# Two rows to a strided product, V laid out with keys adjacent, and softmax scaling moved to ScalarE in a fused attention and two-layer kernel

## The chip, the cores and the metric

The kernel runs on one core of a Trainium2 chip. The metric is the device time of one execution in microseconds. A kernel is run several times and the median is taken; one further execution is recorded by the hardware profiler, and its trace is what the rows below come from. Engines are named PE (TensorE, matmuls), PEld (its weight loads), DVE (VectorE), ACT (ScalarE), POOL (GpSimd) and SP (SyncE, which issues the DMAs here).

## What is computed

Attention on 4 batches, 8 heads, 576 positions, head size 64, and behind it two feed-forward layers on 2304 tokens of 512 values with 2048 hidden units, all in float32. The mask of the first four heads is local, that of the last four strided.

```
scores = (q @ k.T) / sqrt(64)
local  = (rel >= 0) & (rel < 32)                  # heads 0 to 3, rel = query - key
strided = (rel >= 0) & (key % 32 == query % 32)   # heads 4 to 7
attn = exp(where(mask, scores, -1e9) - max); attn /= (sum + 1e-9)
x  = attn @ v                                     # heads side by side: 2304 x 512
y1 = relu(x @ w_in1) ** 2 @ w_out1
h  = y1 @ w_in2;  g = max(h, 0) + alpha * min(h, 0)
out = g @ w_out2
```

## The kernel before

The 2304 tokens form six tiles of 384. Layer 1 goes through tiles 0 to 5, then layer 2 through tiles 0 to 5. A tile has 16 steps, one for each block of 128 hidden units. Matmuls keep float32 precision by splitting a number into a high and a low part (`xh` and `xl`, `gh` and `gl`, two parts of each weight), three products instead of one.

In step n of layer 1, `emit_h(n + 1)` multiplies the next block's first layer into the one PSUM bank `h` (12 matmuls), and `emit_y(n)` multiplies block n's second layer into four banks, first the eight matmuls with `gh`, then the four with `gl`. Between them ScalarE takes `h` out: relu into `g` (line 546), its square as `gh` (547) and once more in full as `g` (548). VectorE makes `gl = g - gh` (line 562). TensorE's next `h` waits for the relu, because there is one bank, and the second part of `y` waits for `gl`.

While the matmuls of tile t run, the attention of tile t + 1 is worked off piece by piece; `plan` and the tables at the top of the file say in which step each piece is emitted. Within a step the order is loads, `emit_gl(n)`, the list `front`, `emit_h(n + 1)`, the list `fill`, the list `tensor_part`, `emit_g(n + 1)`, the list `tail_part`, `emit_y(n)`. The scheduler of the framework may still reorder VectorE's and TensorE's instructions by readiness; SP's order is as written, and ScalarE's too from tile 1's steps on. At the last step `evac` takes the four banks of `y` out, two by ScalarE, two by VectorE.

*Local heads.* A `Unit` handles two heads and three blocks of 64 queries; a tile has four units, put at steps 0, 3, 6 and 9 (in tile 0 at 0, 4, 6 and 9). Its stages are `scores` (TensorE), `softmax_a` (VectorE: mask, maximum, times -scale), `softmax_b` one step later (ScalarE: exp with a sum on the side), `softmax_c` another step later (VectorE: sum plus epsilon, reciprocal, scaling), then `turn`, `turn_copy`, `values` and the emission of `xh` and `xl`. Tile 0's units and its `Dense` units, which do the strided heads of tile 0 by matmul, run ahead of the first step and have buffers of their own.

*Strided heads.* With stride 32 a query sees only the keys of its own residue, at most 18. Residue and head lie on the 128 partitions, and a `Strided` group works on VectorE alone: for a query row i it multiplies the row of q with i + 1 key rows of 64 and sums each product (`score_mul`, `score_sum`), takes the softmax of all rows at once, and multiplies and sums with V (`value_mul`, `value_sum`). In a tile from 2 on a group has 12 rows, i from 6 to 17; tile 1 has two groups, of two rows in two batches and of four rows in two batches. `pieces` cuts a row with more than 9 keys in two; the halves' value sums are then added. `parts` pairs the pieces (two products, then two sums) and `put_strided` spreads the pairs over 14 steps by an estimated cost. V lies in the DRAM as key by key, 64 values each, so that the value product reads operand 0 with keys 64 numbers (256 bytes) apart.

In tile 0's steps VectorE and ScalarE also convert the weights of layer 1 (lines 135 to 163); the last conversion ahead of a step's `h` is line 163.

Of the kernel before, what the change touches and what calls it, by code (L numbers as in the profile page):

```python
# [16 lines left out]
P = 128  # L17
D = 64
# [39 lines left out]
def attn_moe_moe2(  # L58
# [119 lines left out]
    class Unit:  # L178
# [29 lines left out]
        def softmax_a(self):  # L208
            self.e = self.new("e", [P, 3, 96], bufs=1)
            self.st = apool.tile([P, 3, 3], F32, tag="st", name="stat", bufs=4)  # L210
            s = self.s[:, 0:288].rearrange("p (n c) -> p n c", c=96)
            j = 0
            while j < 3:
                k = j
                while k < 3 and self.first[k] == self.first[j]:
                    k += 1
                m = mfirst if self.first[j] else mloc
                nc.vector.tensor_tensor(
                    out=self.e[:, j:k, :], in0=s[:, j:k, :],
                    in1=m.unsqueeze(1).to_broadcast([P, k - j, 96]), op=ALU.add,  # L220
                )
                j = k
            nc.vector.tensor_reduce(out=self.st[:, 0, :], in_=self.e, op=ALU.max, axis=AX.X)
            nc.vector.tensor_scalar(
                out=self.st[:, 0, :], in0=self.st[:, 0, :], scalar1=-SCALE, scalar2=None, op0=ALU.mult
            )

        def softmax_b(self):
            for j in range(3):
                nc.scalar.activation(  # L230
                    out=self.e[:, j, :], in_=self.e[:, j, :], func=AF.Exp, scale=SCALE,
                    bias=self.st[:, 0, j:j + 1], accum_out=self.st[:, 1, j:j + 1],
                )
# [44 lines left out]
    class Dense:  # L278
# [24 lines left out]
        def softmax_a(self):  # L303
            self.e = self.b["e"]
            self.st = apool.tile([P, 3, 3], F32, tag="st", name="stat", bufs=4)
            ms = (mstr.unsqueeze(1), mstr[:, 64:128].unsqueeze(1).to_broadcast([P, 2, 64]))
            for e, sc, m in zip(self.parts(self.e), self.parts(self.s), ms):
                nc.vector.tensor_tensor(out=e, in0=sc, in1=m, op=ALU.add)
            for e, st in zip(self.parts(self.e), (self.st[:, 0, 0:1], self.st[:, 0, 1:3])):
                nc.vector.tensor_reduce(out=st, in_=e, op=ALU.max, axis=AX.X)  # L310
            nc.vector.tensor_scalar(
                out=self.st[:, 0, :], in0=self.st[:, 0, :], scalar1=-SCALE, scalar2=None, op0=ALU.mult
            )

        def softmax_b(self):
            for j, (c, n) in enumerate(SPANS):
                nc.scalar.activation(
                    out=self.e[:, c:c + n], in_=self.e[:, c:c + n], func=AF.Exp, scale=SCALE,
                    bias=self.st[:, 0, j:j + 1], accum_out=self.st[:, 1, j:j + 1],
                )  # L320
# [49 lines left out]
    class Strided:  # L370
# [15 lines left out]
        def load_kv(self, kind):  # L386
            t = spool.tile([P, self.nb, self.a1, D], F32, tag="kv", name="kv", bufs=3)
            src = ks if kind == "k" else vs
            nc.sync.dma_start(
                out=t, in_=src[self.b0:self.b0 + self.nb, :, 0:self.a1, :].rearrange("b p a d -> p b a d")  # L390
            )
            setattr(self, kind, t)
# [4 lines left out]

        def pieces(self, i):

            n = i + 1  # L400
            if self.nb * n <= KCH:
                return [(0, self.nb, 0, n)]
            cuts = [(0, n)] if n <= KCH else [(0, n // 2), (n // 2, n)]
            return [(b, 1, j0, j1) for b in range(self.nb) for j0, j1 in cuts]

        def score_mul(self, i, b, nb, j0, j1):
            n, r = j1 - j0, i - self.a0
            pr = spool.tile([P, nb, n, D], F32, tag="pr", name="pr", bufs=2)
            kb, qb = self.k[:, b:b + nb, j0:j1, :], self.q[:, b:b + nb, r, :]
            if nb == 1:  # L410
                nc.vector.tensor_tensor(  # L411
                    out=pr[:, 0], in0=kb[:, 0],
                    in1=qb.to_broadcast([P, n, D]), op=ALU.mult,
                )
            else:
                nc.vector.tensor_tensor(
                    out=pr, in0=kb, in1=qb.unsqueeze(2).to_broadcast([P, nb, n, D]), op=ALU.mult
                )
            return pr

        def score_sum(self, pr, i, b, nb, j0, j1):
            r = i - self.a0
            if nb == 1:
                nc.vector.tensor_reduce(out=self.s[:, b, r, j0:j1], in_=pr[:, 0], op=ALU.add, axis=AX.X)  # L424
            else:
                nc.vector.tensor_reduce(out=self.s[:, b:b + nb, r, j0:j1], in_=pr, op=ALU.add, axis=AX.X)

        def wide(self, x):
            return x.unsqueeze(2).to_broadcast([P, self.nb * self.n, self.a1])

        def softmax_a(self):
            s = self.s.rearrange("p b n a -> p (b n) a")
# [16 lines left out]

        def value_mul(self, i, b, nb, j0, j1):  # L450
            n, r = j1 - j0, i - self.a0
            pr = spool.tile([P, nb, D, n], F32, tag="pr", name="pr", bufs=2)
            vb, pb = self.v[:, b:b + nb, j0:j1, :], self.s[:, b:b + nb, r, j0:j1]
            if nb == 1:
                nc.vector.tensor_tensor(  # L455
                    out=pr[:, 0], in0=vb[:, 0].rearrange("p a d -> p d a"),
                    in1=pb.to_broadcast([P, D, n]), op=ALU.mult,
                )
            else:
                nc.vector.tensor_tensor(  # L460
                    out=pr, in0=vb.rearrange("p b a d -> p b d a"),
                    in1=pb.unsqueeze(2).to_broadcast([P, nb, D, n]), op=ALU.mult,
                )
            return pr

        def value_sum(self, pr, i, b, nb, j0, j1):
            r = i - self.a0
            if nb > 1:
                nc.vector.tensor_reduce(out=self.o[:, b:b + nb, r, :], in_=pr, op=ALU.add, axis=AX.X)
                return  # L470
            o = self.o[:, b, r, :]
            if j0 == 0:
                nc.vector.tensor_reduce(out=o, in_=pr[:, 0], op=ALU.add, axis=AX.X)  # L473
            else:
                o2 = self.q[:, b, r, :]
# [24 lines left out]
        def parts(self):  # L500

            ps = []
            for kind, mul, add in (
                ("k", self.score_mul, self.score_sum), ("v", self.value_mul, self.value_sum)
            ):
                todo = [(i, pc) for i in range(self.a0, self.a1) for pc in self.pieces(i)]
                for j in range(0, len(todo), 2):

                    def fn(mul=mul, add=add, mine=todo[j:j + 2]):
                        prs = [mul(i, *pc) for i, pc in mine]  # L510
                        for pr, (i, pc) in zip(prs, mine):
                            add(pr, i, *pc)

                    ps.append((sum(134 * pc[1] * (pc[3] - pc[2]) + 140 for _, pc in todo[j:j + 2]), fn, kind))
                if kind == "k":
# [74 lines left out]
    def evac(t, layer):  # L590
# [300 lines left out]
```

## Time and profile before

| | |
|---|---|
| median of 3 runs | 925.78 us (921.92 to 926.69) |
| profiled execution | 927.54 us, of which the recorded span is 925.7 us |
| PE busy | 885.2 us (96%) |
| DVE busy | 613.1 us (66%), 1153 instructions |
| ACT busy | 423.7 us (46%), 939 instructions |
| POOL busy | 1.5 us |

Busy time is the union of an engine's instructions. Matmuls overlap and their ends are modelled, so a busy PE is not one at its peak; a share over the whole span is a mean over stages with different limits. Layer 2 fills the span from 519 us on.

### The profile page before, as it was taken

The page shows a single profiled execution, that of the slowest core. Times are in us where ns is not written, and L with a number is a line of the kernel's source. Part 1 is how long each engine was busy: PE and PEld are TensorE (multiplying, and loading weights), DVE is VectorE, ACT ScalarE, POOL GpSimd, SP SyncE. Part 2 cuts the span into 40 slices and gives each one's busy share as a digit, 9 for nine tenths or more (in the row PEclk, how much of TensorE's full clock was granted, in tenths as well). Part 3 has the DMA queues.
Part 4 walks back from the last instruction along what each step waited for, and adds up shares of the span by engine and source line. Part 5 has one row for each costly group of instructions (what it writes and reads, how often), then busy time and mean ns, then how long its engine had stood idle before and what let it go on. Part 6 is the DMA issues. An engine that isn't in the chain of part 4 may idle for free.

```text
span 925.7 us, 12898 instructions
## 1 busy us (share of the span) xinstructions
PE 885.2 (96%) x4956; PEld 826.6 (89%) x4956; DVE 613.1 (66%) x1153; ACT 423.7 (46%) x939; POOL 1.5 (0%) x10
## 2 busy tenths in 40 slices
PE   7888799989999998999999999999999999999998
PEld 6778689989998998999899999999999999898996
DVE  4899999898898989989578886323233333333222
ACT  4776544434444443543367665333333333434332
POOL 0000000000000000000000000000000000000000
PEclk9999799999999999999999999999999999999999
DMA  9936120213111201210278600100100100100000
GB/s 312 377 123 240 64 71 35 69 33 89 47 54 52 83 22 50 71 55 1 77 255 282 242 4 5 60 10 1 60 10 1 61 9 1 59 9 1 35 1 35
DMA packets 31933, 70.93 MB, mean 77 GB/s; under 512 B 5504, under 2 KB 16256, under 8 KB 31872
## 3 DMA queue, kind: packets, MB, share of 16 engines
q1 hardware_dynamic: 31872, 70.11, 22.2%
q8 instruction: 39, 0.64, 0.3%
q14 instruction: 22, 0.18, 0.1%
HBM read 60.66 MB, written 9.44 MB: 76 GB/s over the span
## 4 chain that ended last, share of the span: by engine, by line
PE 74%; DVE 20%; issue 2%; DMA 1%; ACT 1%; SPq 1%; ACTq 0%
PE ps_h L535 36%; PE ps_y L586 34%; DVE pr L455 7%; DVE so L473 2%; DVE sq L476 2%; DVE gl L562 2%; DVE wt L147 1%; PE ps_s L203 1%; DMA wraw<-in_w1i_dram 1%; DVE w L163 1%; DVE wt L144 1%; PE ps_pt L246 1%; PE ps_y L348 1%; DVE so L477 1%; DMA dense_qk<-in_qd_dram 1%
## 5 line engine op out<-in xcount | busy, mean ns | idle before, releaser
L535 PE MATMUL ps_h<-xh,w 128*128 128x384 f32 x1536 | 433.3, 343 | 7.9 <-ACT w L157 3.3
L535 PEld LDWEIGHTS ps_h<-xh,w 128*128 128x128 f32 x1536 | 287.3, 192 | 15.5 <-ACT w L157 4.4
L535 PE MATMUL ps_h<-xl,w 128*128 128x384 f32 x768 | 262.0, 341 | 0.0
L553 DVE SCALAR_TENSOR_TENSOR g<-u,nalpha,g 128x384 f32<-128x384 f32 x96 | 59.3, 618 | 193.6 <-ACT u L552 193.6
L562 DVE TENSOR_TENSOR gl<-g,gh 128x384 fp32r<-128x384 f32 x192 | 106.3, 553 | 76.6 <-ACT gh L556 49.1
L586 PE MATMUL ps_y<-gh,w 128*128 128x384 f32 x768 | 155.1, 343 | 0.0
L535 PEld LDWEIGHTS ps_h<-xl,w 128*128 128x128 f32 x768 | 147.3, 192 | 4.1
L546 ACT ACTIVATE g<-ps_h 128x384 f32<-128x384 f32 x96 | 47.2, 492 | 224.4 <-PE ps_h L535 208.4
L586 PE MATMUL ps_y<-w,gh 128*128 128x512 f32 x576 | 149.0, 394 | 0.1
L586 PEld LDWEIGHTS ps_y<-gh,w 128*128 128x128 f32 x768 | 135.3, 191 | 1.1
L551 ACT ACTIVATE g<-ps_h 128x384 f32<-128x384 f32 x96 | 47.2, 492 | 168.3 <-PE ps_h L535 168.1
L586 PEld LDWEIGHTS ps_y<-w,gh 128*128 128x128 f32 x576 | 106.6, 188 | 17.3 <-ACT gh L556 0.6
L586 PE MATMUL ps_y<-gl,w 128*128 128x384 f32 x384 | 85.5, 344 | 16.1 <-DVE gl L562 16.1
L586 PEld LDWEIGHTS ps_y<-gl,w 128*128 128x128 f32 x384 | 68.6, 192 | 20.2 <-DVE gl L562 20.0
L455 DVE TENSOR_TENSOR pr<-kv,ss 128x384 f32<-128x384 f32 (+4 forms) x92 | 85.1, 949 | 0.1
L556 ACT ACTIVATE gh<-g 128x384 fp32r<-128x384 f32 x96 | 50.5, 526 | 69.0 <-DVE g L553 69.0
L586 PE MATMUL ps_y<-w,gl 128*128 128x512 f32 x288 | 82.0, 392 | 0.0
L586 PEld LDWEIGHTS ps_y<-w,gl 128*128 128x128 f32 x288 | 54.1, 188 | 12.5
L411 DVE TENSOR_TENSOR pr<-kv,sq 128x384 f32<-128x384 f32 (+4 forms) x92 | 54.8, 616 | 0.0
L424 DVE TENSOR_REDUCE ss<-pr 128x6 f32<-128x384 f32 (+4 forms) x92 | 53.3, 611 | 0.1
L547 ACT ACTIVATE gh<-g 128x384 fp32r<-128x384 f32 x96 | 50.5, 526 | 3.0
L548 ACT ACTIVATE g<-g 128x384 f32<-128x384 f32 x96 | 50.5, 526 | 2.9
(103 smaller groups left out, 654.6 us busy)
## 6 DMA issues: line engine op xcount, KB each, us to landing
wraw<-in_w1i_dram SPq DMA_DIRECT2D x16, 512.0 KB, 7.7
wraw<-in_w1o_dram SPq DMA_DIRECT2D x16, 512.0 KB, 7.8
wraw<-in_w2i_dram SPq DMA_DIRECT2D x16, 512.0 KB, 3.6
wraw<-in_w2o_dram SPq DMA_DIRECT2D x16, 512.0 KB, 4.5
qk<-in_qk_dram SPq DMA_DIRECT2D x20, 336.0 KB, 4.1
y<-ev SPq DMA_DIRECT2D x24, 192.0 KB, 2.0
x2raw<-y SPq DMA_DIRECT2D x24, 192.0 KB, 3.3
out_dram<-ev SPq DMA_DIRECT2D x18, 256.0 KB, 2.3
```

The costliest lines, as they stand in the source:

```text
L411: nc.vector.tensor_tensor(out=pr[:, 0], in0=kb[:, 0], in1=qb.to_broadcast([P, n, D]), op=ALU.mult,)
L424: nc.vector.tensor_reduce(out=self.s[:, b, r, j0:j1], in_=pr[:, 0], op=ALU.add, axis=AX.X)
L455: nc.vector.tensor_tensor(out=pr[:, 0], in0=vb[:, 0].rearrange("p a d -> p d a"), in1=pb.to_broadcast([P, D, n]), op=ALU.mult,)
L535: nc.tensor.matmul(h[:, 0:T], a, b[:, c, :], start=(c == 0 and i == 0), stop=(c == NC - 1 and i == 2))
L546: nc.scalar.activation(out=g, in_=h[:, 0:T], func=AF.Relu)
L547: nc.scalar.activation(out=gh, in_=g, func=AF.Square)
L548: nc.scalar.activation(out=g, in_=g, func=AF.Square)
L551: nc.scalar.activation(out=g, in_=h[:, 0:T], func=AF.Relu)
L553: nc.vector.scalar_tensor_tensor(out=g, in0=u, scalar=nalpha[:, f:f + 1], in1=g, op0=ALU.mult, op1=ALU.add)
L556: nc.scalar.activation(out=gh, in_=g, func=AF.Copy)
L562: nc.vector.tensor_tensor(out=gl, in0=g, in1=gh.bitcast(F32), op=ALU.subtract)
L586: nc.tensor.matmul(y, a, b, start=(f == 0 and i == 0), stop=(f == NF - 1 and i == 2))
```

## The change

Three things, all in layer 1 and the attention beside it.

1. A strided product takes two query rows of one batch at once (`ROWS = 2`). Both rows get the key count of the later one; the score that the earlier row gets too much is overwritten with -1e30 by `later`, a VectorE memset ahead of the softmax, so that its probability is zero. A row pair of more than 9 keys is cut over the keys for the scores and over the 64 values for V, so that no halves are added any more. The product buffers `pr` grow from 576 to 1,152 numbers a partition. V is laid out value by value with the keys adjacent (`vs`, and `vs1` for tile 1's six keys).
2. In the softmax of the local heads and of `Dense` the mask's addition multiplies by the scale too, and the maximum is written negated, so that the small multiplication behind it goes. In `softmax_c` of tiles 1 to 5 three ScalarE activations scale by the reciprocal, in place of one VectorE multiplication.
3. All four `evac` copies of layer 1 are ScalarE's.

The launch also asks for a smaller scratch area for dynamic DMAs, which makes room for the larger buffers; no DMA of the kernel is issued from POOL.

```diff
-                nc.vector.tensor_tensor(
-                    out=self.e[:, j:k, :], in0=s[:, j:k, :],
-                    in1=m.unsqueeze(1).to_broadcast([P, k - j, 96]), op=ALU.add,
+                nc.vector.scalar_tensor_tensor(
+                    out=self.e[:, j:k, :], in0=s[:, j:k, :], scalar=SCALE,
+                    in1=m.unsqueeze(1).to_broadcast([P, k - j, 96]), op0=ALU.mult, op1=ALU.add,
                 )
                 j = k
-            nc.vector.tensor_reduce(out=self.st[:, 0, :], in_=self.e, op=ALU.max, axis=AX.X)
-            nc.vector.tensor_scalar(
-                out=self.st[:, 0, :], in0=self.st[:, 0, :], scalar1=-SCALE, scalar2=None, op0=ALU.mult
-            )
+            nc.vector.tensor_reduce(out=self.st[:, 0, :], in_=self.e, op=ALU.max, axis=AX.X, negate=True)
...
-            nc.vector.tensor_tensor(
-                out=self.e, in0=self.e, in1=r.unsqueeze(2).to_broadcast([P, 3, 96]), op=ALU.mult
-            )
+            if self.t == 0:
+                nc.vector.tensor_tensor(
+                    out=self.e, in0=self.e, in1=r.unsqueeze(2).to_broadcast([P, 3, 96]), op=ALU.mult
+                )
+                return
+            for j in range(3):
+                nc.scalar.activation(
+                    out=self.e[:, j, :], in_=self.e[:, j, :], func=AF.Copy, scale=r[:, j:j + 1]
+                )
...
+            if kind == "k":
+                t = spool.tile([P, self.nb, self.a1, D], F32, tag="kv", name="kv", bufs=3)
+                src = ks[b:e, :, 0:self.a1, :].rearrange("b p a d -> p b a d")
+            else:
+                t = spool.tile([P, self.nb, D, self.a1], F32, tag="kv", name="kv", bufs=3)
+                src = (vs1 if self.t == 1 else vs)[b:e].rearrange("b p d a -> p b d a")
...
+        def pieces(self, kind):
+
+            ps = []
+            for b in range(self.nb):
+                for r in range(0, self.n, ROWS):
+                    n = self.a0 + r + ROWS
+                    full = n if kind == "k" else D
+                    cuts = [(0, full)] if n <= KCH else [(0, full // 2), (full // 2, full)]
+                    ps += [(b, r, n, c0, c1) for c0, c1 in cuts]
+            return ps
...
+            nc.vector.tensor_tensor(
+                out=pr, in0=self.k[:, b, j0:j1, :].unsqueeze(1).to_broadcast([P, ROWS, m, D]),
+                in1=self.q[:, b, r:r + ROWS, :].unsqueeze(2).to_broadcast([P, ROWS, m, D]), op=ALU.mult,
+            )
...
+        def later(self):
+
+            for b in range(self.nb):
+                flat = self.s[:, b].rearrange("p n a -> p (n a)")
+                nc.vector.memset(flat[:, self.a0 + 1::ROWS * (self.a1 + 1)], NEG)
...
-            vb, pb = self.v[:, b:b + nb, j0:j1, :], self.s[:, b:b + nb, r, j0:j1]
-            if nb == 1:
-                nc.vector.tensor_tensor(
-                    out=pr[:, 0], in0=vb[:, 0].rearrange("p a d -> p d a"),
-                    in1=pb.to_broadcast([P, D, n]), op=ALU.mult,
-                )
...
+            nc.vector.tensor_tensor(
+                out=pr, in0=self.v[:, b, d0:d1, 0:n].unsqueeze(1).to_broadcast([P, ROWS, m, n]),
+                in1=self.s[:, b, r:r + ROWS, 0:n].unsqueeze(2).to_broadcast([P, ROWS, m, n]), op=ALU.mult,
+            )
...
+                    cost = 0
+                    for b, r, n, c0, c1 in todo[j:j + 2]:
+                        cost += 134 * ROWS * ((c1 - c0) if kind == "k" else n * (c1 - c0) // D) + 310
+                    ps.append((cost, fn, kind))
...
-            if o % 2 == 0:
+            if o % 2 == 0 or layer == 0:
                 nc.scalar.activation(out=ev, in_=y[:, 0:cols], func=AF.Copy)
```

The lines of the changed kernel shift: `gl` is line 554 there, the score product 418 and its sum 425, the value product 459 and its sum 466, the transposes 474, the sum plus epsilon 236, the reciprocal 237, the exp 229, ScalarE's scaling 244, relu and squares 538 to 540.

VectorE's order in step 2 of a tile whose strided work is a 12-row group, where the first unit's softmax ends (`stat` holds its sums and reciprocals, `pr` the products, `ss` the scores). Before:

```order
L562 TENSOR_TENSOR gl<-g,gh 128x384
L424 TENSOR_REDUCE ss<-pr 128x6
L237 TENSOR_SCALAR stat<-stat 128x3
L411 TENSOR_TENSOR pr<-kv,sq 128x448
L238 RECIPROCAL stat<-stat 128x3
L411 TENSOR_TENSOR pr<-kv,sq 128x448
L239 TENSOR_TENSOR e<-e,stat 128x288
L424 TENSOR_REDUCE ss<-pr 128x7 x2
```

After:

```order
L554 TENSOR_TENSOR gl<-g,gh 128x384
L236 TENSOR_SCALAR stat<-stat 128x3
L418 TENSOR_TENSOR pr<-kv,sq 128x896
L237 RECIPROCAL stat<-stat 128x3
L418 TENSOR_TENSOR pr<-kv,sq 128x1024
L425 TENSOR_REDUCE ss<-pr 128x2x7
L425 TENSOR_REDUCE ss<-pr 128x2x8
```

The scaling (line 239) has left VectorE, and the product between sum and reciprocal has twice the elements.

ScalarE's order at the same kind of place, the fourth unit of the last strided tile (`xh` is a unit's output, `e` the exponentials). Before:

```order
L265 ACTIVATE xh_4108<-ps_o 128x192
L230 ACTIVATE e,stat<-e,stat 128x96 x3
L546 ACTIVATE g<-ps_h 128x384
L547 ACTIVATE gh<-g 128x384
L548 ACTIVATE g<-g 128x384
```

After:

```order
L270 ACTIVATE xh_3868<-ps_o 128x192
L229 ACTIVATE e,stat<-e,stat 128x96 x3
L244 ACTIVATE e<-e,stat 128x96 x3
L538 ACTIVATE g<-ps_h 128x384
L539 ACTIVATE gh<-g 128x384
L540 ACTIVATE g<-g 128x384
```

The three scalings stand between the exponentials and the next step's relu.

VectorE's order at the end of a 12-row tile (`so` holds the value sums, `ot` their transposes). Before:

```order
L562 TENSOR_TENSOR gl<-g,gh 128x384
L455 TENSOR_TENSOR pr<-kv,ss 128x512 x2
L476 TENSOR_REDUCE sq<-pr 128x64
L473 TENSOR_REDUCE so<-pr 128x64
L477 TENSOR_TENSOR so<-so,sq 128x64
L455 TENSOR_TENSOR pr<-kv,ss 128x576 x2
L476 TENSOR_REDUCE sq<-pr 128x64
L473 TENSOR_REDUCE so<-pr 128x64
L477 TENSOR_TENSOR so<-so,sq 128x64
L562 TENSOR_TENSOR gl<-g,gh 128x384
L455 TENSOR_TENSOR pr<-kv,ss 128x576
```

After:

```order
L466 TENSOR_REDUCE so<-pr 128x2x32 x2
L554 TENSOR_TENSOR gl<-g,gh 128x384
L459 TENSOR_TENSOR pr<-kv,ss 128x1152
L474 STREAM_TRANSPOSE ot<-so 128x384
L466 TENSOR_REDUCE so<-pr 128x2x32
L554 TENSOR_TENSOR gl<-g,gh 128x384
L474 STREAM_TRANSPOSE ot<-so 128x384
L554 TENSOR_TENSOR gl<-g,gh 128x384
```

Between two `gl` there stood four value products with their sums and additions; now one product with its sum and a transpose.

## Rows read from the trace of the kernel before

**Rows 1.** Stretches in us: busy us (instructions) by engine, granted clock, DMA share, GB/s.
```profile
45.00:126.50 81.50, 65.96 (x370) 59.82 (x369) 80.43 (x139) 51.40 (x97) 0.28 (x1) 0.90 0.39 144
...
219.70:298.20 78.50, 75.60 (x470) 73.40 (x469) 73.08 (x151) 33.30 (x85) 0.28 (x1) 0.98 0.19 56
...
455.20:519.00 63.80, 63.80 (x370) 63.80 (x369) 46.46 (x58) 41.92 (x66) 0.00 (x0) 1.00 0.76 260
519.00:925.70 406.70, 402.18 (x2017) 363.79 (x2015) 155.27 (x247) 164.20 (x337) 0.00 (x0) 1.00 0.08 29
```

**Rows 2.** Waits, 219.7 to 298.2 us: us in total, times, longest.
```profile
PE ps_y L586 <- DVE gl L562: 2.9, 2, 2.3
```

**Rows 3.** Timeline of PE: start, us, instructions, idle before.
```profile
286.67 0.98 PE L586 MATMUL ps_y<-gl,w 128*128 128x384 f32 x4 [2.28 <-DVE gl L562]
```

**Rows 4.** Stretch behind that wait, columns as in rows 1.
```profile
287.60:291.00 3.40, 3.40 (x13) 3.40 (x12) 2.84 (x7) 0.00 (x0) 0.28 (x1) 0.51 0.36 110
```

**Rows 5.** Timeline of PE in the last tile of layer 1.
```profile
452.33 1.55 PE L586 MATMUL ps_y<-gh,w 128*128 128x384 f32 x8
453.72 0.85 PE L586 MATMUL ps_y<-gl,w 128*128 128x384 f32 x4
...
456.49 1.55 PE L586 MATMUL ps_y<-gh,w 128*128 128x384 f32 x8
```

**Rows 6.** Groups by line, DVE: busy us, mean ns of one, idle before.
```profile
L455 DVE TENSOR_TENSOR pr<-kv,ss 128x384 f32<-128x384 f32 (+4 forms) x92 | 85.1, 949 | 0.1
...
L411 DVE TENSOR_TENSOR pr<-kv,sq 128x384 f32<-128x384 f32 (+4 forms) x92 | 54.8, 616 | 0.0
L424 DVE TENSOR_REDUCE ss<-pr 128x6 f32<-128x384 f32 (+4 forms) x92 | 53.3, 611 | 0.1
...
L473 DVE TENSOR_REDUCE so<-pr 128x64 f32<-128x320 f32 (+4 forms) x56 | 32.7, 596 | 0.0
L476 DVE TENSOR_REDUCE sq<-pr 128x64 f32<-128x384 f32 (+4 forms) x36 | 22.4, 623 | 0.1
...
L477 DVE TENSOR_TENSOR so<-so,sq 128x64 f32<-128x64 f32 x36 | 7.7, 213 | 0.1
```

**Rows 7.** Timeline of DVE: two instructions in a row.
```profile
103.96 2.35 DVE L163 TENSOR_TENSOR w<-wt,w 128x1024 fp32r<-128x1024 f32 x2
```

**Rows 8.** Groups by line and shape, DVE, columns as in rows 6.
```profile
L144 DVE SCALAR_TENSOR_TENSOR wt<-wraw 128x1024 uint32<-128x1024 uint32 x29 | 35.2, 1218 | 1.0 <-DMA wraw<-in_w2o_dram 0.5 <-ACT wraw L135 0.5
...
L163 DVE TENSOR_TENSOR w<-wt,w 128x1024 fp32r<-128x1024 f32 x29 | 35.2, 1221 | 4.6 <-ACT w L157 4.6
...
L455 DVE TENSOR_TENSOR pr<-kv,ss 128x576 f32<-128x576 f32 x16 | 18.6, 1181 | 0.0
...
L411 DVE TENSOR_TENSOR pr<-kv,sq 128x576 f32<-128x576 f32 x16 | 11.9, 749 | 0.0
...
L239 DVE TENSOR_TENSOR e<-e,stat 128x288 f32<-128x288 f32 x20 | 8.9, 447 | 0.0
...
L224 DVE TENSOR_SCALAR stat<-stat 128x3 f32<-128x3 f32 x24 | 3.8, 160 | 0.1
...
L460 DVE TENSOR_TENSOR pr<-kv,ss 128x384 f32<-128x384 f32 x1 | 0.6, 596 | 0.0
```

**Rows 9.** Groups by line and shape, ACT, columns as in rows 6.
```profile
L230 ACT ACTIVATE e<-e,stat 128x96 f32<-128x96 f32 x60 | 21.6, 364 | 0.1
...
L604 ACT ACTIVATE ev<-ps_y 128x384 f32<-128x384 f32 x12 | 5.2, 488 | 0.0
...
L495 ACT ACTIVATE xh<-ot 128x128 fp32r<-128x128 f32 x2 | 0.5, 304 | 0.5 <-DVE ot L485 0.5
```

**Rows 10.** Timeline of ACT: a step's relu and second square.
```profile
253.67 0.49 ACT L546 ACTIVATE g<-ps_h 128x384 f32<-128x384 f32 x1 [2.92 <-PE ps_h L535]
...
254.75 0.53 ACT L548 ACTIVATE g<-g 128x384 f32<-128x384 f32 x1
```

**Rows 11.** Chain that ended last, around 125 us: start, us, what.
```profile
125.36 1.14 DVE w L163
```

More of the change, by code (lines that the diff above doesn't have):

```diff
@@ L31 @@
 GROUPS = [[], [(0, 2, 4, 6), (2, 2, 2, 6)]] + [[(b, 1, 6, 18)] for b in range(4)]
+ROWS = 2
 KCH = 9
@@ L65, in attn_moe_moe2 @@
     vs: bass.AP,
+    vs1: bass.AP,
     w_in1: bass.AP,
@@ L230, in softmax_b @@
                 nc.scalar.activation(
-                    out=self.e[:, j, :], in_=self.e[:, j, :], func=AF.Exp, scale=SCALE,
+                    out=self.e[:, j, :], in_=self.e[:, j, :], func=AF.Exp,
                     bias=self.st[:, 0, j:j + 1], accum_out=self.st[:, 1, j:j + 1],
@@ L307, in softmax_a @@
             for e, sc, m in zip(self.parts(self.e), self.parts(self.s), ms):
-                nc.vector.tensor_tensor(out=e, in0=sc, in1=m, op=ALU.add)
+                nc.vector.scalar_tensor_tensor(out=e, in0=sc, scalar=SCALE, in1=m, op0=ALU.mult, op1=ALU.add)
             for e, st in zip(self.parts(self.e), (self.st[:, 0, 0:1], self.st[:, 0, 1:3])):
-                nc.vector.tensor_reduce(out=st, in_=e, op=ALU.max, axis=AX.X)
-            nc.vector.tensor_scalar(
-                out=self.st[:, 0, :], in0=self.st[:, 0, :], scalar1=-SCALE, scalar2=None, op0=ALU.mult
-            )
+                nc.vector.tensor_reduce(out=st, in_=e, op=ALU.max, axis=AX.X, negate=True)
         def softmax_b(self):
@@ L317, in softmax_b @@
                 nc.scalar.activation(
-                    out=self.e[:, c:c + n], in_=self.e[:, c:c + n], func=AF.Exp, scale=SCALE,
+                    out=self.e[:, c:c + n], in_=self.e[:, c:c + n], func=AF.Exp,
                     bias=self.st[:, 0, j:j + 1], accum_out=self.st[:, 1, j:j + 1],
@@ L386, in load_kv @@
         def load_kv(self, kind):
[L387 to L391, printed above, removed]
+            b, e = self.b0, self.b0 + self.nb
+            if kind == "k":
[4 more added lines that the diff above has]
+                src = (vs1 if self.t == 1 else vs)[b:e].rearrange("b p d a -> p b d a")
+            nc.sync.dma_start(out=t, in_=src)
             setattr(self, kind, t)
@@ L396, in fill @@
             nc.gpsimd.memset(self.s, NEG)
[L398 to L409, printed above, removed]
-            if nb == 1:
-                nc.vector.tensor_tensor(
[L412 to L418, printed above, removed]
-            return pr
@@ L421, in score_sum @@
[L421 to L426, printed above, removed]
+        def pieces(self, kind):
[7 more added lines that the diff above has]
+            return ps
@@ new lines, in score_mul, with score_sum @@
+        def score_mul(self, b, r, n, j0, j1):
+            m = j1 - j0
+            pr = spool.tile([P, ROWS, m, D], F32, tag="pr", name="pr", bufs=2)
+            nc.vector.tensor_tensor(
+                out=pr, in0=self.k[:, b, j0:j1, :].unsqueeze(1).to_broadcast([P, ROWS, m, D]),
+                in1=self.q[:, b, r:r + ROWS, :].unsqueeze(2).to_broadcast([P, ROWS, m, D]), op=ALU.mult,
+            )
+            return pr
+        def score_sum(self, pr, b, r, n, j0, j1):
+            nc.vector.tensor_reduce(out=self.s[:, b, r:r + ROWS, j0:j1], in_=pr, op=ALU.add, axis=AX.X)
@@ L431, in softmax_a @@
         def softmax_a(self):
+            self.later()
             s = self.s.rearrange("p b n a -> p (b n) a")
@@ L505, in parts @@
             ):
-                todo = [(i, pc) for i in range(self.a0, self.a1) for pc in self.pieces(i)]
+                todo = self.pieces(kind)
                 for j in range(0, len(todo), 2):
                     def fn(mul=mul, add=add, mine=todo[j:j + 2]):
[L510 to L514, printed above, removed]
+                        prs = [mul(*pc) for pc in mine]
+                        for pr, pc in zip(prs, mine):
+                            add(pr, *pc)
+                    cost = 0
+                    for b, r, n, c0, c1 in todo[j:j + 2]:
+                        cost += 134 * ROWS * ((c1 - c0) if kind == "k" else n * (c1 - c0) // D) + 310
+                    ps.append((cost, fn, kind))
                 if kind == "k":
@@ L864 @@
         "vl": vl.reshape(NTILE, 2, 2, 96, 3, 2 * D_),
-        "qs": residues(q), "ks": residues(k), "vs": residues(v),
+        "qs": residues(q), "ks": residues(k),
+        "vs": residues(v).transpose(0, 1, 3, 2), "vs1": residues(v)[:, :, :6].transpose(0, 1, 3, 2),
         "w1i": slots(w1), "w1o": w1o.reshape(DFF // P, P, DM),
```

30 lines of the change are left out of this document (6 added, 24 removed).

## Prediction

> **What bounds the kernel now.** I read the table of stretches first, then the waits of the stage it points at, then single rows. The table [rows 1] splits the execution. From 519 us on (layer 2) TensorE is busy without a break and the change touches nothing, so that stretch cannot move; nor can the last tile of layer 1 (455 to 519), 63.8 of 63.8 us busy. From 45 to 126.5 us (tile 0) VectorE is the bound: 80.4 of 81.5 us. Between lie four tiles of 78.5 us each, of which [rows 1] shows one; the other three are alike to 0.1 us. There TensorE works 75.6 us and VectorE 73.1, so neither is simply full.
>
> What ends last in such a tile is told by its waits: TensorE waits for `gl` alone, twice, 2.9 us in all [rows 2], the longer time for 2.28 us at 286.67 [rows 3]. Behind that wait the granted clock is 0.51, thus the lower level of 1.2 GHz, for 3.4 us [rows 4], in which TensorE does 1.7 us less work. So a tile loses 2.9 + 1.7 = 4.6 us because VectorE comes late, and TensorE's own work is 78.5 - 4.6 = 73.9 us. Per step that is 4.16 us (from one step's start of `y` to the next [rows 5]); 16 make 66.6, and 7.3 are the attention matmuls, 1.8 a unit.
>
> So the change can win at most 4 x 4.6 = 18.4 us in these tiles, and whatever it takes off VectorE ahead of 126.5 us.
>
> **The change part by part.** *Strided products.* Before, the five strided tiles issue 92 products and 92 sums for the scores, 92 value products, 56 + 36 value sums and 36 additions [rows 6], with 8 more in forms of two batches. Count times mean: 56.7 + 56.2 + 87.3 + 33.4 + 22.4 + 7.7 + 5.4 (the 8, taken at about 0.68) = 269 us in 412 instructions. Two in a row overlap: two of 1.22 take 2.35 [rows 7], so 0.08 comes off each, 236 us remain.
>
> After, a 12-row tile has per pass 11 pieces (8, 5+5, 6+6, 7+7, 8+8, 9+9 keys, each of two rows of 64), 9,984 elements; tile 1 has 6 pieces, 4,096 elements. Four passes: 200 instructions, 176,128 elements. The trace has no piece over 1,024 elements. From 576 elements at 749 ns to 1,024 at 1,221 [rows 8] the line is 1.054 ns an element and 0.142 us an instruction: 185.6 + 28.4 = 214 us, less 0.08 x 200 = 198. So 38 us go, 1.8 of them in tile 1 (its 40 instructions cost 20.6 us by the same rows, its 24 new ones 18.8): 9.0 us in each 12-row tile. Where they come from: 3.0 from 49 fewer instructions a tile, 7 from the value product, and 1.6 are given back for a key too many in every other row.
>
> The value product is the term with an open price. Reading V with keys 256 bytes apart took 1,181 ns for 576 elements where the score product took 749; V now lies with keys adjacent. I take the score product's rate, since the 384-element value product of three keys, whose probabilities are repeated 64 times just as now, took 596 [rows 8]: repeated short rows cost nothing there. The other bound is the old rate, 7.5 us more a tile (rival B).
>
> *Masks and maxima.* The mask's addition becomes a scalar-tensor-tensor with the scale; at 1,024 elements both forms take 1.22 [rows 7, 8], so nothing is charged. The multiplication behind the maximum goes: 160 ns [rows 8], 0.08 behind overlap, 4 units a tile: 0.3. The added memset of six elements is 0.1 a tile, an estimate from the same row.
>
> *Scaling to ScalarE.* VectorE loses 447 ns [rows 8], 0.37 behind overlap: 1.5 a tile. ScalarE gets three activations of 96 elements with a per-partition scale. Between 304 ns (128 elements, immediate scale) and 364 (96 elements, per-partition bias) [rows 9] I take 364; with the same overlap the three take 0.9. The Trainium skill, "ScalarE: Activation LUTs", Rules for kernel authors, says that multiplications belong on VectorE, not ScalarE; by its figures (186 + 93 for a pointer operand + 0.833 a column) one takes an estimated 359 ns, so three take 0.9 again; left on VectorE, as the rule would have it, the scaling would make VectorE's load below 63.9 instead of 62.4 and rival C would not exist. No row here shows a scaling on ScalarE yet. What decides is which engine the tile waits for: VectorE is busy 73.1 of 78.5 us, ScalarE 33.3 [rows 1].
>
> *Evacuation.* Two copies more on ScalarE, 0.49 each [rows 9]. All four start when tile t's last `y` ends, and the new tile's first `y` comes behind an `h`, half a step or 2.1 us later, bank by bank; four take 2.0. No charge; without that cover it would be up to 1 us a tile. What VectorE saves by it I leave out.
>
> VectorE's load in a 12-row tile: 73.1 - 9.0 - 0.3 + 0.1 - 1.5 = 62.4 of TensorE's 73.9 us. Enough on average; but the pieces are larger, so I walked a tile by the new order. Let E(n) be the end of `h` of step n. Both squares are done at E + 1.7 (relu at 253.67 to 255.28, and 0.1 ahead of it [rows 10]), so `gl` is ready to start there; TensorE needs it at E + 4.16 + 1.39 [rows 5] plus the attention matmuls between. With E(0) = 0: VectorE ends `gl` of step 0 at 2.6 (needed at 6.3), of step 1 at 6.7 (10.4), of step 2 at 12.2 (14.6), of step 3 at 17.4 (20.1), and in the value half of step 8 at 40.0 (43.5), of step 11 at 55.0 (57.9), of step 12 at 61.1 (62.7), of step 13 at 64.7 (67.4). No deadline is missed; the tightest has 1.6 us.
>
> The new wait is ScalarE's. Its three scalings stand ahead of the next step's relu, and wait for VectorE's reciprocal, which has a strided product ahead of it. In step 2: `gl` done 12.2, exp done 12.4, sum plus epsilon, product of 896 (1.0), reciprocal to 13.6, scalings to 14.6, relu to 15.1. TensorE wants the bank of `h` at E(3) + 2.08 = 15.3. 0.2 us to spare, the same at unit 3 (58.4 against 58.6); at the other two units about 0.7. Since these gaps are as small as my errors, I charge 0.3 us a tile: 4.3 us won, 17.2 in four.
>
> *Tile 0.* VectorE's work up to the last conversion that `h` waits for (125.36 [rows 11]): 4 multiplications -0.3, 4 scalings -1.5, value products of the first group -0.95, two-row pieces of the second group +0.8 (an extra key for each second row, and three-key products that were cheap already), memsets +0.3: about -1.6 us. VectorE's conversions wait for ScalarE's there, and ScalarE's scalings, ahead of some of them, can lengthen that.
>
> Sum: 17.2 + 1.6 = 18.8. The profiled execution took 927.54 us, 1.8 above the median of the runs shown: 908.7 in its terms, 907 as a median.
>
> **The rivals.** *B, the value product stays slow*, because its price hangs on something other than the key step. Then the value half carries 7.5 us more: `gl` of step 12 moves from 61.1 to about 67, over 4 us late, and the lower clock comes with it. Against: the three-key row. All that is left is tile 0: 927.5 - 1.6 - 1.8 = 924.
>
> *C, ScalarE's scalings hold the relu* (the other side, slower). Each unit has one place, and all sixteen in four tiles are alike. If VectorE is later there than I walked by x, TensorE stands x - 0.2 to x - 0.7. Up to about 1.6 us late the gain of 18.8 pays for it (16 x 1.15 = 18.4); beyond that it is slower, and at 2 us, with the lower clock behind each (1.7), 16 x (1.5 + 1.7) - 18.8 = 32 us slower: 958. For it: the product between sum and reciprocal; against: VectorE is caught up at three of the four units. The rule of the Trainium skill named above ("ScalarE: Activation LUTs", Rules for kernel authors) speaks for this rival.
>
> *D, part of the waits stay*: the tight step 12, or pieces of 1,152 elements above my line. Half of 4.6 a tile is won, 9.2 in four, and tile 0's 1.6: 915 as a median.
>
> *E, tile 0 wins more*, as fewer small instructions let TensorE keep its clock there (0.90 [rows 1]): 5 to 7 us more, 901.
>
> *F, the change does nothing*: VectorE would have to be off the path, which the waits exclude; it is within B.
>
> **How the numbers follow.** Forecast A 0.68, D 0.12, E 0.07, B 0.07, C 0.06. A alone spans 904 to 912 (all of 18.4 and 3 in tile 0, or 14 and nothing). For 8 in 10: D's centre and E's above and below: 900 to 917. Runs of before scatter by 0.5%, which is what a measurement here can tell. Faster: A, D, E, 0.87; within 0.5%: most of B, 0.06; slower: C and the rest, 0.07.
>
> **What would show it.** Value products of 1,152 elements near 1.36 us and equal to score products; VectorE near 61 us in tiles of about 74; no wait of TensorE for `gl` over 0.7 us and a granted clock of 1.0 from 141 us to the end; layer 2 unchanged at 402 us of TensorE; tile 0 ending 1 to 2 us earlier. Wrong would be: relu on ScalarE waiting for the reciprocal with TensorE idle before `h` (C), value products at 2.2 us (B), or new waits for a conversion before 126 us that eat the gain.

## The result and the profile after

The changed kernel takes 903.29 us as a median of 4 runs (902.84 to 905.1), the kernel before 925.72 (921.92 to 926.69, 4 runs): a ratio of 0.9769 (0.9738 to 0.9799), 22.4 us less. The profiled executions are 902.84 and 927.54 us, 24.7 apart.

The same stretches of the changed kernel as in [rows 1], with the end of tile 0 as a row of its own (busy us by engine, granted clock, DMA share, GB/s):

```profile
45.00:123.50 78.50, 62.97 (x371) 56.40 (x369) 78.47 (x123) 53.98 (x109) 0.28 (x1) 0.98 0.41 152
123.50:136.72 13.22, 13.19 (x76) 13.19 (x77) 12.76 (x21) 5.86 (x13) 0.28 (x1) 1.00 0.12 36
...
209.62:283.06 73.44, 73.44 (x470) 71.98 (x469) 61.19 (x93) 37.29 (x100) 0.28 (x1) 1.00 0.21 60
...
429.94:496.90 66.96, 66.96 (x388) 66.96 (x387) 47.46 (x60) 44.83 (x74) 0.00 (x0) 1.00 0.77 260
496.90:901.10 404.20, 399.63 (x2002) 361.19 (x2000) 153.08 (x243) 163.10 (x335) 0.00 (x0) 1.00 0.08 27
```

The four tiles between tile 0 and the last tile of layer 1 are called steady tiles here. One is now 73.44 us long (the first 72.9, as it was shorter before too), TensorE is busy in all of it at a clock of 1.00, and from 136.7 us to the end its waits view is empty. VectorE works 61.2 us of the tile. Taken from the start of one tile's evacuation to the next one's, tile 0 ends at 136.20 instead of 140.74 (4.5 us), the four steady tiles last 293.2 instead of 313.4 (20.1 us), and what follows is unchanged (471.7 against 471.6). Behind 126.5 us the kernel before had needed this for the end of tile 0 (same view):

```profile
126.50:141.20 14.70, 14.66 (x75) 14.66 (x76) 13.91 (x27) 5.79 (x13) 0.28 (x1) 0.88 0.06 20
```

The new operations by line and shape (busy us, mean ns, idle before), VectorE's first, then ScalarE's:

```profile
L418 DVE TENSOR_TENSOR pr<-kv,sq 128x1152 f32<-128x1152 f32 x8 | 10.8, 1350 | 0.0
...
L459 DVE TENSOR_TENSOR pr<-kv,ss 128x1152 f32<-128x1152 f32 x8 | 10.7, 1340 | 0.0
...
L220 DVE SCALAR_TENSOR_TENSOR e<-ps_s,mloc 128x288 f32<-128x288 f32 x20 | 9.0, 450 | 11.6 <-PE ps_s L205 11.6
...
L431 DVE MEMSET ss<- 128x6 f32 x4 | 0.3, 63 | 0.1
```
```profile
L244 ACT ACTIVATE e<-e,stat 128x96 f32<-128x96 f32 x60 | 18.3, 366 | 21.2 <-DVE stat L237 20.9
```

The value product runs at the score product's rate, 1.34 us for 1,152 elements. The scalings wait for the reciprocal 20.9 us in all, yet nobody waits for them. Unit 0 of a steady tile shows why: timeline of ScalarE, then of TensorE.

```profile
220.61 0.91 ACT L244 ACTIVATE e<-e,stat 128x96 f32<-128x96 f32 x3 [1.38 <-DVE stat L237]
221.43 0.47 ACT L538 ACTIVATE g<-ps_h 128x384 f32<-128x384 f32 x1
```
```profile
221.90 0.85 PE L578 MATMUL ps_y<-gl,w 128*128 128x384 f32 x4
222.59 0.33 PE L527 MATMUL ps_h<-xh,w 128*128 128x384 f32 x1
```

The relu ends at 221.90, the next `h` wants its bank at 222.59: 0.69 us to spare. By the same reading units 1 to 3 have 1.36, 1.39 and 1.06. The tightest `gl` (266.29 to 266.84) is 2.1 us ahead of its matmuls at 268.98.

### The profile page after: what moved, and what is told of

It reads as the page before. It is cut to its first block, busy times and chain, and to the rows that moved or that the text cites. A ratio compares the mean times of both kernels' runs of the same rounds, so it can differ in the third digit from the quotient of the medians.

```text
span 901.1 us, 12704 instructions
## 1 busy us (share of the span) xinstructions
PE 872.2 (97%) x4956; PEld 815.6 (91%) x4956; DVE 559.0 (62%) x889; ACT 444.1 (49%) x1011; POOL 1.5 (0%) x10
## 4 chain that ended last, share of the span: by engine, by line
PE 88%; DVE 8%; issue 1%; DMA 1%; ACT 1%; SPq 0%; ACTq 0%; DVEq 0%
PE ps_y L578 42%; PE ps_h L527 41%; DVE wt L146 2%; DVE wt L149 1%; PE ps_s L205 1%; DVE w L165 1%; PE ps_o L261 1%; PE ps_pt L251 1%; DVE wraw L145 1%; PE ps_y L350 1%; DMA qk<-in_qk_dram 1%; DVE gl L554 1%; DMA first_qk<-in_qk_dram 1%; DVE ss L425 0%; DVE so L466 0%
## 5 line engine op out<-in xcount | busy, mean ns | idle before, releaser
L527 PE MATMUL ps_h<-xh,w 128*128 128x384 f32 x1536 | 427.0, 338 | 11.3 <-ACT w L159 5.9
L527 PEld LDWEIGHTS ps_h<-xh,w 128*128 128x128 f32 x1536 | 281.6, 189 | 19.2 <-ACT w L159 6.9
L527 PE MATMUL ps_h<-xl,w 128*128 128x384 f32 x768 | 258.1, 336 | 0.0
L527 PEld LDWEIGHTS ps_h<-xl,w 128*128 128x128 f32 x768 | 144.9, 189 | 4.1
L578 PEld LDWEIGHTS ps_y<-gh,w 128*128 128x128 f32 x768 | 133.1, 188 | 1.1
L578 PE MATMUL ps_y<-gl,w 128*128 128x384 f32 x384 | 83.2, 337 | 4.9 <-DVE gl L554 4.9
L459 DVE TENSOR_TENSOR pr<-kv,ss 128x768 f32<-128x768 f32 (+5 forms) x50 | 52.1, 1065 | 0.1
L418 DVE TENSOR_TENSOR pr<-kv,sq 128x768 f32<-128x768 f32 (+5 forms) x50 | 51.9, 1066 | 0.0
L425 DVE TENSOR_REDUCE ss<-pr 128x12 f32<-128x768 f32 (+5 forms) x50 | 51.8, 1061 | 0.0
```

The lines of the kernel that those rows point to most:

```text
L418: nc.vector.tensor_tensor(out=pr, in0=self.k[:, b, j0:j1, :].unsqueeze(1).to_broadcast([P, ROWS, m, D]), in1=self.q[:, b, r:r + ROWS, :].u ...
L425: nc.vector.tensor_reduce(out=self.s[:, b, r:r + ROWS, j0:j1], in_=pr, op=ALU.add, axis=AX.X)
L459: nc.vector.tensor_tensor(out=pr, in0=self.v[:, b, d0:d1, 0:n].unsqueeze(1).to_broadcast([P, ROWS, m, n]), in1=self.s[:, b, r:r + ROWS, 0: ...
L527: nc.tensor.matmul(h[:, 0:T], a, b[:, c, :], start=(c == 0 and i == 0), stop=(c == NC - 1 and i == 2))
L578: nc.tensor.matmul(y, a, b, start=(f == 0 and i == 0), stop=(f == NF - 1 and i == 2))
```

## The experiments

The kernels below were measured in three groups, each beside the kernel before, whose median was 927.08, 925.51 and 926.17 us there (925.72 beside the changed kernel). A ratio is to the kernel before in the same group. Medians of different groups can differ by 1 to 2 us for that reason alone; the length of the steady tiles tells more.

**Which part wins the steady tiles.** Three kernels take the change apart. The first keeps only the strided part:

```diff
-                nc.vector.scalar_tensor_tensor(out=self.e[:, j:k, :], ..., scalar=SCALE, ...)
+                nc.vector.tensor_tensor(out=self.e[:, j:k, :], ..., op=ALU.add)   # and maximum, times -SCALE
-            for j in range(3): nc.scalar.activation(... scale=r[:, j:j + 1])
+            nc.vector.tensor_tensor(out=self.e, in0=self.e, in1=r..., op=ALU.mult)
-            if o % 2 == 0 or layer == 0:
+            if o % 2 == 0:
```

> The strided part alone (row pairs, V with keys adjacent); softmax of the local heads and evacuation as before. Theory 1, VectorE was late by its strided products and nothing else of the change is needed in the steady tiles: four tiles of 73.4 us instead of 78.5 (20.2 us gained), tile 0 ends 0.7 to 2.2 us earlier, 903 to 906 us in all. Theory 2, the parts that went to ScalarE are needed too: a wait for gl and the lower clock behind it stay in each tile, 910 us or more.

904.48 us (901.32 to 905.86), ratio 0.9747 (0.9719 to 0.9775), steady tiles of 73.44 us (columns as above):

```profile
211.27:284.71 73.44, 73.44 (x470) 71.98 (x469) 63.73 (x103) 33.28 (x87) 0.28 (x1) 1.00 0.20 60
```

The strided part alone gives the whole gain there: theory 1. Its ratio is no worse than the 0.9769 of the whole change, so the other two parts show no gain in the whole time either.

The second keeps everything else of the change (the scale in the mask's addition, the negated maximum, scaling and evacuation on ScalarE), with the strided part of before.

> The rest of the change without the strided part: scale in the mask's addition, negated maximum, scaling on ScalarE, four evacuations on ScalarE. Theory 1: behind VectorE's last idle time in a tile of before, two units' scalings and negations lie ahead of the late gl, 0.9 us; the short wait goes, the 2.28 us wait and the lower clock stay, 0.9 a tile; tile 0 gains 2 to 3 us; 919 to 922 us. Theory 2 (the ScalarE parts win half of it): 915 us or less.

926.26 us, ratio 0.9994 (0.998 to 1.0007): no gain at all, less than either theory gave. The four steady tiles of its profile last 312.9 us, against 313.4 before. The waits for `gl` are gone from the steady tiles, but in each TensorE now stands once for the relu, and the clock falls behind it. Timeline of TensorE, of ScalarE, and the stretch behind the wait:

```profile
275.83 0.69 PE L535 MATMUL ps_h<-xh,w 128*128 128x384 f32 x1 [2.72 <-ACT g L546]
```
```profile
274.50 0.91 ACT L242 ACTIVATE e<-e,stat 128x96 f32<-128x96 f32 x3 [5.75 <-DVE stat L235]
275.31 0.47 ACT L546 ACTIVATE g<-ps_h 128x384 f32<-128x384 f32 x1
```
```profile
275.50:279.00 3.50, 3.17 (x10) 3.17 (x11) 3.50 (x7) 1.32 (x3) 0.00 (x0) 0.55 0.01 2
```

ScalarE had waited 5.75 us for the reciprocal of unit 3, with the relu queued behind the scalings. That is rival C, in the kernel in which VectorE is late. So the third leaves the scaling on VectorE and keeps mask, maximum and evacuation:

```diff
-            for j in range(3): nc.scalar.activation(... scale=r[:, j:j + 1])
+            nc.vector.tensor_tensor(out=self.e, in0=self.e, in1=r..., op=ALU.mult)
```

> The kernel before with the scale in the mask's addition, the negated maximum and the four evacuations on ScalarE; strided part and scaling as before. Theory 1, the scaling on ScalarE holds relu only while VectorE is late, so that in the run with the rest of the change one wait merely took another's place: here the waits for gl are back, 2 to 2.9 us a tile, no wait for relu, steady tiles of 78.2 to 78.5 us, 923 to 926.5 us in all. Theory 2, ScalarE's load as such makes the wait for relu: it stays here, and without the scaling's 0.9 us it is 1.8 us.

921.26 us, ratio 0.9957 (0.9934 to 0.998), 5.0 us less than with the scaling moved, or 4.1 if each is taken against the kernel before in its group. The steady tiles, which the scatter of tile 0 does not touch, differ more: four of them last 306.4 us here and 312.9 there. The wait for the relu is gone and those for `gl` are back, as theory 1 has it, but the tile is 76.8 us long, better than its 78.2, and the whole is below its range. Waits and stretch of one tile:

```profile
PE ps_y L580 <- DVE gl L556: 2.4, 3, 1.2
```
```profile
217.50:294.30 76.80, 74.36 (x470) 71.92 (x469) 71.79 (x145) 34.06 (x88) 0.28 (x1) 1.00 0.20 58
```

Three short waits (0.49, 0.72 and 1.24 us) stand where two of 0.63 and 2.28 were, and the clock stays at 1.00. The tile is 3.3 us over 73.44, of which the waits are 2.45: each costs 0.3 us beyond what the view shows. Which of mask, maximum and evacuation wins the 7.0 us against the four tiles of before is not shown.

**Layout or pairing.** V key by key again, with row pairs:

```diff
-                in0=self.v[:, b, d0:d1, 0:n].unsqueeze(1).to_broadcast([P, ROWS, m, n]),
+                in0=self.v[:, b, 0:n, d0:d1].rearrange("p a d -> p d a").unsqueeze(1).to_broadcast([P, ROWS, m, n]),
```

> The whole change, but V stays key by key in memory, so that the value product of a row pair reads keys 256 bytes apart. Theory 1, the price hangs on the key step: a value product of 1152 elements takes 2.2 to 2.4 us, 7.5 us more on VectorE in each 12-row tile; with the 2.1 us to spare that the changed kernel shows at gl of step 12, TensorE then waits over 4 us in each tile, and the clock falls behind it: 922 to 930 us. Rival, the price hung on the number of instructions or on the probabilities' repetition: products of 1152 elements take 1.4 us and the time is 903 to 905 us.

931.45 us, ratio 1.0049 (1.0027 to 1.007), above the kernel before and above the range expected. Only V's layout differs from the changed kernel, and a value product takes 2,169 ns in place of 1,340:

```profile
L455 DVE TENSOR_TENSOR pr<-kv,ss 128x1152 f32<-128x1152 f32 x8 | 17.4, 2169 | 0.0
```

The place of the wait was not the expected one: in its tile TensorE stands 0.71 us for `gl` and 2.66 for the relu behind the scalings.

```profile
278.68 0.69 PE L523 MATMUL ps_h<-xh,w 128*128 128x384 f32 x1 [2.66 <-ACT g L534]
```

VectorE is busy 68.4 us of this tile of 79.2, against 73.1 of 78.5 in the kernel before, and yet the tile is longer. VectorE's lateness comes out where the tightest link is. The counterpart has single rows and the new layout:

```diff
-ROWS = 2
+ROWS = 1
-            self.later()
```

> The change with single rows (ROWS = 1), V with keys adjacent. Theory 1, the layout pays and the pairing is worth little: 40 more instructions a tile at 0.06 us against 1,536 elements fewer at 1.05 ns, VectorE about 0.9 us fuller a tile, nothing late: 903 to 905 us. Rival, the pairing is needed: VectorE 5 us fuller a tile and a wait for gl in each, 910 us or more.

904.0 us, ratio 0.9772 (0.9741 to 0.9803), steady tiles of 73.44 us, VectorE busy 62.1 us of one. A value product of 576 elements takes 749 ns, which [rows 8] gave for the score product of that size. Theory 1: the layout pays, and the pairing is worth 0.9 us of VectorE a tile that nothing needs. The new layout by itself, with neither the pairing nor the parts on ScalarE, was not run.

**The other parts, undone one by one.** The scaling back on VectorE (the diff above, on the changed kernel):

> The change with the scaling left on VectorE (one multiplication in place of three on ScalarE). Theory 1: the steady tiles have 2 us to spare at every gl and stay at 73.4 us; tile 0, where VectorE is full, ends 1.5 us later, and up to 3 us later if TensorE's clock falls again behind it: 904.8 to 906.5 us. The rule that multiplications belong on VectorE: 903 us or less.

904.84 us (904.29 to 905.2), steady tiles of 73.44 us. The steady tiles don't feel the scaling on either engine. The median is 1.5 us above the changed kernel's, but the kernel before stood 1.4 us higher in this group, and the ratio is 0.9755 (0.9735 to 0.9776): a loss in tile 0 is not shown.

> The change with the four copies of layer 1's evacuation split between ScalarE and VectorE as before. Theory 1 (and the prediction): no tile changes, 73.4 us each, 901 to 905 us with the scatter of tile 0. Rival, one engine alone holds the banks of the next tile's first y: tiles shorter by up to 1 us, 899 us.

903.47 us; its steady tiles are 73.60 us, 0.16 longer than with four ScalarE copies, the opposite of the rival. With two copies (1.01 us) back on VectorE, unit 0's reciprocal comes 0.9 us later in the tile, ScalarE's scalings wait 2.27 us for it in place of 1.38, and `h` can only start as the relu behind them ends, 0.24 us later than in the changed kernel (timeline of ScalarE, then of TensorE):

```profile
295.26 0.91 ACT L244 ACTIVATE e<-e,stat 128x96 f32<-128x96 f32 x3 [2.27 <-DVE stat L237]
296.07 0.47 ACT L538 ACTIVATE g<-ps_h 128x384 f32<-128x384 f32 x1
```
```profile
296.59 0.45 PE L527 MATMUL ps_h<-xh,w 128*128 128x384 f32 x1
```

The kernel with the strided part alone splits the copies too, but scales on VectorE, and its tiles are 73.44 us. So the split costs something only together with the scaling on ScalarE.

> The change with mask's addition, maximum and the multiplication by -scale as before. Theory 1 (and the prediction): steady tiles stay at 73.4 us, as VectorE has 2 us to spare; tile 0 ends 0.3 to 0.6 us later: 903 to 906 us. Rival, the scalar-tensor-tensor form from PSUM costs more than the addition did: 902 us or less.

905.17 us (901.01 to 905.58), steady tiles of 73.44. Neither this kernel nor the one with the split copies is told from the changed kernel by the whole time.

**How much room the relu has.** ScalarE gets 3 or 6 activations more behind the scalings of tiles 2 to 5, with a result that is not used:

```diff
+            if self.t > 1:
+                junk = apool.tile([P, 96], F32, tag="junk", name="junk", bufs=1)
+                for j in range(3):                       # or 6
+                    nc.scalar.activation(out=junk, in_=self.e[:, j % 3, :], func=AF.Copy, scale=r[:, j % 3:j % 3 + 1])
```

> The changed kernel with three more ScalarE activations of 96 elements behind the three scalings in the units of tiles 2 to 5 (their result is not used), so that relu starts 0.8 us later. Theory 1, from the trace after (relu ends 0.69, 1.36, 1.39 and 1.06 us ahead of TensorE's next h): only the first unit stands, 0.1 us and a restart: 0.4 a tile, 903.5 to 905.5 us. Theory 2, by the prediction's walk (0.2 and 0.7 to spare): 2.6 us a tile, 911 to 914 us.

905.11 us (904.35 to 907.7); steady tiles of 73.9, 0.45 longer than the changed kernel's.

> The same with six more activations, relu 1.6 us later. Theory 1: all four units stand, 0.95, 0.28, 0.25 and 0.58 us with 0.28 of restart each, 3.2 us a tile, without a lower clock as each wait is short: 914 to 918 us. Theory 2, by the prediction's walk: 5 us a tile and the lower clock behind some: 923 us or more.

914.09 us (913.91 to 914.32); steady tiles of 76.2, 2.75 longer. Both are theory 1's: the prediction's 0.2 us of room was too little, the 0.69 to 1.39 read from the trace is right. Unit 0's wait is the longest (1.56 us where 0.95 was expected, since TensorE takes score matmuls first and then stands), and the clock stays at 1.00 behind it:

```profile
227.43 0.44 PE L531 MATMUL ps_h<-xh,w 128*128 128x384 f32 x1 [1.56 <-ACT g L542]
```
```profile
227.50:231.00 3.50, 3.50 (x20) 3.50 (x21) 3.50 (x5) 2.08 (x5) 0.00 (x0) 1.00 0.00 0
```

**What a late `gl` costs.** One long VectorE reduction ahead of a `gl` in each steady tile:

```diff
+    def late(n, m):
+        gl = g_sb[n][1][:, 0:128].bitcast(F32)
+        nc.vector.tensor_reduce(out=junk[:, 0:m], in_=gl.unsqueeze(1).to_broadcast([P, m, 128]), op=ALU.max, axis=AX.X)
+    for t, m in zip((1, 2, 3, 4), (54, 58, 62, 67)):
+        at(fill, t * NF + 13, late, t * NF + 13, m)
```

> The changed kernel with one VectorE reduction more in each of the four steady tiles, of 54, 58, 62 and 67 rows of 128 (its result is not used), ahead of gl of step 14, so that gl comes late by about 0.7, 1.2, 1.8 and 2.4 us. Theory 1, a wait costs its idle time, 0.28 us of restart on top, and 1.6 us where the granted clock falls behind it: the tiles are longer by 1.0, 1.5, 2.0 and 2.7 us, plus 1.6 for each behind which the clock falls (the last at least, as in the kernel before), 8.8 to 13.6 us in all: 912 to 917 us. Theory 2, as the prediction counted it (idle time and clock alone): 6.1 to 10.9 us, 909 to 914 us, and no tile longer than idle plus clock.

907.96 us, below both ranges. It does not decide: the tiles are 0.7, 0.25, 0.5 and 1.2 us longer, since the scheduler, which knew of the long reduction, put four matmuls of the next `h` and the score matmuls ahead of the late `gl`. Only the last tile shows a wait (1.41 us), without a lower clock.

**A version that beats both?** With TensorE full from 136.7 us on, tile 0 is what is left, and VectorE is full there. Tile 1's twelve products on GpSimd, their sums one place later:

```diff
-            nc.vector.tensor_tensor(out=pr, ...)
+            (nc.gpsimd if self.t == 1 else nc.vector).tensor_tensor(out=pr, ...)      # both products
```

> The change with tile 1's twelve strided products (768 and 512 elements, worked off during tile 0) on GpSimd instead of VectorE, each pair's sums a place later in the order. With the steady tiles at TensorE's own time, only tile 0 can still be shortened. Theory 1: VectorE loses 8.3 us of products there, tile 0 ends 4 to 8 us earlier: 895 to 900 us. Rival, GpSimd takes several times as long for a product, VectorE's sums stand in order ahead of conversions and wait for it: 903 us or more.

909.91 us, 6.6 more than the changed kernel: the rival's time. Tile 0 ends at 142.57. GpSimd's groups, and what its last four products did to two conversions on VectorE (two in a row take 2.35 us otherwise [rows 7]):

```profile
L459 POOL TENSOR_TENSOR pr<-kv,ss 128x768 f32<-128x768 f32 x4 | 10.0, 2503 | 39.5 <-DVE ss L453 39.5
L418 POOL TENSOR_TENSOR pr<-kv,sq 128x768 f32<-128x768 f32 x4 | 7.7, 1938 | 30.7 <-DMA kv<-in_ks_dram 30.7
```
```profile
122.15 7.90 POOL L459 TENSOR_TENSOR pr<-kv,ss 128x512 f32<-128x512 f32 x4 [26.73 <-DVE ss L453]
```
```profile
127.06 4.08 DVE L165 TENSOR_TENSOR w<-wt,w 128x1024 fp32r<-128x1024 f32 x2
```

The rival's reason holds in part: GpSimd takes 2.0 to 2.7 times as long, but VectorE's sums wait for it only 1.1 and 0.8 us. What the rival did not have is that VectorE's own instructions take longer while GpSimd works.

## Why the prediction was right, and where its sizes were off

*The bound and the maximal gain.* The mechanism was right: VectorE came late by its strided products, TensorE stood for `gl` and lost its clock behind it, and all of it is gone. The term that was mis-sized is "a tile loses 2.9 + 1.7 = 4.6 us". It measured 5.1 (78.5 to 73.44), so that four tiles gave 20.1 us, more than the 18.4 called the most. The waits view counts from the modelled end of the last matmul, and the next would have started before that end. In the kernel before the step of [rows 3] begins like this on TensorE:

```profile
282.73 1.67 PE L586 MATMUL ps_y<-gh,w 128*128 128x384 f32 x8
```

And in the changed kernel:

```profile
267.50 1.64 PE L578 MATMUL ps_y<-gh,w 128*128 128x384 f32 x8
268.98 0.85 PE L578 MATMUL ps_y<-gl,w 128*128 128x384 f32 x4
```

From 282.73 to 286.67 are 3.94 us; in the changed kernel the same two groups start 1.48 apart. That is 2.46 lost, where the view shows 2.28, and the four matmuls behind the wait took 0.98 instead of 0.85. So a wait costs its idle time and 0.3 us (2.46 + 0.13 - 2.28). Two waits a tile with 2.9 of idle, 0.6 for the two and 1.6 for the clock make 5.1. The three waits without a lower clock in the kernel with mask and evacuation alone give the same 0.3 by themselves.

*Strided products.* Right in size: 1,152 elements at 1.34 and 1.35 us (1.36 predicted), and VectorE at 61.2 us of a steady tile (62.4). The open price was settled for the value product by layout alone: 2,169 ns with the old one, 1,340 with the new. The three-key row that the prediction trusted could not separate the two causes, and that it led to the right rate was partly luck. It too read V with keys 256 bytes apart, and took 596 ns against 548 for the score product of its size, while the four-key product beside it paid the price in full, 1,089 against 682:

```profile
L460 DVE TENSOR_TENSOR pr<-kv,ss 128x512 f32<-128x512 f32 x1 | 1.1, 1089 | 0.0
```

Why three keys were cheap is not known. Of the 3.0 us a tile credited to 49 fewer instructions, less 1.6 for the extra keys, the single-row kernel, which has 40 of them back, shows 0.9 on VectorE (62.1 against 61.2); it was worth nothing in time. Rival B described the layout's part well, and understated it: with the slow product the kernel is not at 924 but at 931.

*Scaling on ScalarE and the new wait.* The scalings took 366 ns each (364 taken). The estimate of 359 by the figures of the Trainium skill ("ScalarE: Activation LUTs", What ACT_TABLE_LOAD costs) agrees with that to 2%. The charge of 0.3 us a tile was not needed: the walk left 0.2 us of room, the trace shows 0.69 or more and the kernels with three and six more activations confirm it. But rival C was more than a small chance of something going wrong; it is what the same edit does where VectorE is late. Alone with mask and evacuation it takes back 6.5 of the 7.0 us that these win in the steady tiles, and in the kernel with row pairs and the old layout TensorE stands 2.66 us a tile for the relu behind it. The Trainium skill, "ScalarE: Activation LUTs", Rules for kernel authors, keeps multiplications on VectorE. In that kernel the trace agrees with keeping this one there (steady tiles of 78.4 against 76.8 us), but by what is queued behind the scalings, not by the speed of an element; in the changed one the steady tiles are 73.44 us either way.

*Mask, maximum, evacuation.* No charge, and none seen: the scalar-tensor-tensor from PSUM takes 450 ns and the memset 63. Split copies cost 0.16 us a tile beside the scaling on ScalarE, and nothing in the kernel with the strided part alone.

*Tile 0.* In the two profiles it ends 4.5 us earlier, not 1.6. VectorE's busy time up to the last conversion fell by 2.0 us (80.4 to 78.5), its idle time by 1.0, and the matmuls behind that conversion ran at a clock of 1.00 instead of 0.88, 1.5 us. Rival E named the clock, which was a smaller part; that fewer instructions raised it is not shown. As a median over runs less is left: 22.4 less the 20.1 of the tiles is 2.3 us. Kernels that differ from the changed one only in later tiles ended tile 0 at 136.2 and 136.5 (six and three activations more), but 139.1 (the late `gl`), with the clock at 0.85 from 100 to 123 us. So one profile's tile 0 does not tell a part of 1 or 2 us, and which edit wins how much there stays open.

*Sum.* 17.2 + 1.6 was predicted, 20.1 + 4.5 is what the profiles show and 20.1 + 2.3 the medians. 903.29 is in the range of 900 to 917, but 0.7 below the 904 to 912 that forecast A spans alone, since its most, 18.4, was itself too small.

## What to carry to other kernels

Price a wait of TensorE from the distance between starts of the same instructions with and without it, and add the stretch at the lower clock behind it, for the waits view alone shows too little. Before work goes from a late engine to one with spare time, look at what that second engine does next: its queue waits in order for the late engine's result, and may hold something that was never late. An operand read with a large step is worth a new layout ahead of any fusing of instructions: here single rows with the new layout had all of the steady gain, and row pairs with the old layout had none.

## What the runs showed of the hardware

- Behind waits of TensorE of 1.24, 1.41 and 1.56 us the granted clock stayed at 1.00; behind 2.28 us [rows 3, 4], 2.66 and 2.72 us it fell to 0.51 to 0.55, the lower level of 1.2 GHz, for about 3.4 us. So three short waits with 2.45 us of idle cost 3.3, two with 2.9 cost 5.1.
- A product of 1,152 elements on VectorE takes 2,169 ns with an operand whose innermost step is 256 bytes, 1,340 with adjacent numbers: 0.72 ns more an element. With four or five keys, at 512 and 320 elements, it was 0.80 and 0.75; with three keys, at 384 elements, 0.12 (596 ns against 548).
- GpSimd took 1.9 to 2.5 us for products of 768 elements (0.95 on VectorE), and two VectorE subtractions beside its work took 4.08 us instead of 2.35. The Trainium skill, "Perfetto Trace Analysis", Optimizing Scalar/DVE Operations, says that the two share a read port of SBUF, so that moving work between them may not help; here it cost 6.6 us.
